# Gated decode attention: one ring for all loads, V as the stationary operand, and stages interleaved per 512 rows

## The chip, the cores and the metric

One core of a Trainium2 chip runs the kernel. A core has TensorE (PE: matmuls; its weight loads are listed as PEld), VectorE (DVE), ScalarE (ACT), GpSimd (POOL), SyncE (SP, which here issues the transfers) and 16 DMA engines. The metric is the device time of one execution in microseconds. No other core runs. The profile also gives TensorE's granted clock as a share of full speed. Ratios below are the record's ratios of fast runs with their 95% intervals, so they are not quite the ratio of the medians that are quoted.

## The reference, cut to what matters

```python
B, Sq, D = 2, 1, 448;  Hq, Hkv, Sk, Dh = 16, 8, 32768, 256;  F = 1792     # all bf16
q = (x @ wq) per head                                # one query row per batch entry
scores = einsum("bhqd,bhkd->bhqk", q, k) * Dh**-0.5  # two query heads share one K/V head
p = softmax(scores);  o = einsum("bhqk,bhkd->bhqd", p, v);  a = o @ wo
b = gelu(x @ w1 + b1) @ w2 + b2
g = sigmoid((x * gate_w).sum(-1));  out = g * a + (1 - g) * b
```

K and V are 268 MB each, and every byte is used once, for two query heads. So 537 MB must be moved, and TensorE must see all of it: K twice (a transpose, then the score product), V once. There are 16 groups (batch x K/V head) with 8 tiles of 4096 rows (2 MB) each of K and of V.

## The kernel before

A *step* takes one K tile through stages A and B, and one V tile, eleven steps behind, through stage C. Each stage runs over the whole tile before the next one begins.

```python
NBK = NBV = 4        # 4 buffers of 2 MB for K, 4 for V; wq, w1, w2 lie in V's at the start
NKT = 2; NPB = 3     # 2 buffers for a transposed K tile, 3 PSUM banks for transposes
...
def A(kt):                                   # 32 f32 transposes, two bf16 columns at a time
    wait_tile(E, ("K", kt))
    for bl in range(8):                      # 4 transposes to one bank, copied as 128x512
        E.wait(evac_eng(...), ("E", ...))    # the copy that empties this bank, ACT or DVE by turns
        for i in range(4): transpose(bank[:, i*P:(i+1)*P], KV[slot][:, r, :].bitcast(f32), ident_f)
def B(kt):                                   # 64 matmuls of 2 columns: KT is the weights
    for r in range(32):
        for j in range(2):
            matmul(pss[:, t*R + r, :], buf[:, j, r*P:(r+1)*P], qT_sb[:, kvh, j, :, b], ...)
def C(vt):                                   # 32 matmuls of 256 columns: P is the weights, V streams
    for r in range(32):
        matmul(ps_o[g % 2][0:2, 0:Dh], pt[:, t*R + r, :], KV[slot][:, r, :], ...)
...
for s in range(NSTEP + 1):
    A(s); B(s - 1); ...; C(s - DELTA)        # DELTA = 8 + 3
```

SyncE issues x (element by element), K tile 0, wq, K tile 1, the small weights and biases, then K and V tiles by turns, each when the last user of its buffer is done.

## Time and profile before

| | before |
|---|---|
| time, median of 4 | 1371.09 us (1369.15 to 1375.18); of the first 3, which the prediction knew, 1371.68; later medians of 7, 1369.57 to 1371.15 |
| profiled span | 1367.6 us |
| PE busy, granted clock | 93%, 0.980 |
| transfers | 549.8 MB, mean 402 GB/s |
| PE waiting for a transfer | 17 us, all before 50 us (14.5 for K, 1.7 for the gate weights, 1.0 for wq) |

These lines are from the profile's page of the kernel before. PE and PEld give busy time. The rows of 40 digits are equal slices of the span: the granted clock in tenths, the busy share of the DMA engines, and GB/s. Then follow the chain of waits by engine (it goes back from the last instruction, at each step to what released it), and the costliest groups of instructions with busy time, mean ns of one, and idle time ahead of them.

```profile
span 1367.6 us, 36510 instructions
...
PE 1269.7 (93%) x16778; PEld 1035.4 (76%) x16778; DVE 682.2 (50%) x1144; ACT 564.4 (41%) x1126; POOL 1.2 (0%) x9
...
PEclk7899999999999999999999999999999999999999
DMA  8989999999999999999999999999999999999876
GB/s 277 414 356 427 426 426 426 427 426 425 413 415 407 407 419 404 420 413 415 401 402 419 407 419 417 407 419 409 405 409 410 418 405 414 427 426 425 338 272 289
...
PE 73%; DVE 12%; ACT 10%; SPq 2%; issue 1%; DMA 1%; DVEq 0%
...
L414 PE MATMUL psT<-ident_f,KV 128*128 128x128 f32 x4096 | 565.3, 282 | 90.9 <-ACT KT L596 39.6
...
L477 PE MATMUL ps_o<-KV,PT 128*2 128x256 bf16 x4096 | 480.1, 277 | 0.0
...
L440 PE MATMUL ps_s<-qT_sb,KT 128*128 128x2 bf16 x8192 | 223.0, 163 | 0.0
```

All of DMA reads 9 tenths and so does PE, so neither row says which of them is the limit. The chain does: 73% PE, 22% copies, 1% DMA. The next lines are the chain in order of time for one step (start, duration, what):

```profile
212.34 0.60 PE psT L414 x4
...
212.96 1.08 ACT KT L596 x2
...
216.13 1.09 PE psT L414 x8
217.22 1.58 PE ps_s L440 x64
218.80 3.58 PE ps_o L477 x32
222.38 0.60 PE psT L414 x4
```

Transposes and the copies that they wait for take 4.9 us, scores 1.6, the value product 3.6; the step is 10.04 us. The windows of the same kernel (stretch, its length, busy time with count on PE, PEld, DVE, ACT and POOL, clock, DMA share, GB/s):

```profile
120.00:200.00 80.00, 75.35 (x1023) 61.82 (x1021) 42.48 (x71) 34.85 (x69) 0.00 (x0) 1.00 1.01 425
400.00:800.00 400.00, 377.31 (x5039) 307.95 (x5038) 207.09 (x347) 169.46 (x337) 0.00 (x0) 0.99 1.00 411
```

425 GB/s were moved from 120 to 200 us, and 411 later (413 from 800 to 1200 us).

### The profile page before, as it was taken

What the parts mean: (1) busy time and instruction counts of PE and PEld (TensorE: products, weight loads), DVE (VectorE), ACT (ScalarE), POOL (GpSimd) and SP (SyncE); (2) the same over time, 40 slices, a digit from 0 to 9 for tenths busy, and PEclk for the clock granted to TensorE, in tenths of its full rate; (3) what the DMA queues carried; (4) which work ended last, traced back from release to release, by engine and by line L of the source; (5) the groups of instructions that cost most, each with busy time, mean ns of one, the idle gap of its engine ahead of it and who ended that gap; (6) DMA issues with size and microseconds to landing.
All of it is one profiled execution on the core that took longest, in us unless ns stands there. A gap on an engine that the chain in (4) does not pass through costs nothing.

```text
span 1367.6 us, 36510 instructions
## 1 busy us (share of the span) xinstructions
PE 1269.7 (93%) x16778; PEld 1035.4 (76%) x16778; DVE 682.2 (50%) x1144; ACT 564.4 (41%) x1126; POOL 1.2 (0%) x9
## 2 busy tenths in 40 slices
PE   5898999999999999999999999999999999999998
PEld 5777777777777777777777777777777777777776
DVE  1575455455445545545545545455445545545520
ACT  2555344444434434444334434344344434444410
POOL 0000000000000000000000000000000000000000
PEclk7899999999999999999999999999999999999999
DMA  8989999999999999999999999999999999999876
GB/s 277 414 356 427 426 426 426 427 426 425 413 415 407 407 419 404 420 413 415 401 402 419 407 419 417 407 419 409 405 409 410 418 405 414 427 426 425 338 272 289
DMA packets 47664, 549.78 MB, mean 402 GB/s; under 512 B 7508, under 2 KB 13400, under 8 KB 14744
## 3 DMA queue, kind: packets, MB, share of 16 engines
q1 hardware_dynamic: 47512, 547.45, 97.1%
q8 instruction: 132, 2.16, 0.6%
q14 instruction: 20, 0.16, 0.0%
HBM read 547.43 MB, written 0.00 MB: 400 GB/s over the span
## 4 chain that ended last, share of the span: by engine, by line
PE 73%; DVE 12%; ACT 10%; SPq 2%; issue 1%; DMA 1%; DVEq 0%
PE ps_o L477 34%; PE psT L414 22%; PE ps_s L440 14%; DVE KT L666 12%; ACT KT L596 10%; DMA KV<-in_A_k_cache_dram 1%; SPq L270 1%; PE ps_m L492 1%; PE ps_s L504 0%; PE ps_m L451 0%; SPq L266 0%; PE ps_m L458 0%; PE ps_s L389 0%; ACT z_sb L577 0%; SPq L259 0%
## 5 line engine op out<-in xcount | busy, mean ns | idle before, releaser
L666 DVE COPY KT<-psT 128x512 bf16<-128x512 bf16 x1024 | 647.0, 685 | 546.1 <-PE psT L414 534.3
L596 ACT COPY KT<-psT 128x512 bf16<-128x512 bf16 x1024 | 537.9, 595 | 713.8 <-PE psT L414 713.6
L414 PE MATMUL psT<-ident_f,KV 128*128 128x128 f32 x4096 | 565.3, 282 | 90.9 <-ACT KT L596 39.6
L414 PEld LDWEIGHTS psT<-ident_f,KV 128*128 128x128 f32 x4096 | 443.1, 142 | 206.9 <-DVE KT L666 95.7
L477 PE MATMUL ps_o<-KV,PT 128*2 128x256 bf16 x4096 | 480.1, 277 | 0.0
L477 PEld LDWEIGHTS ps_o<-KV,PT 128*2 128x2 bf16 x4096 | 340.6, 85 | 108.0 <-DMA KV<-in_A_v_cache_dram 0.2
L440 PEld LDWEIGHTS ps_s<-qT_sb,KT 128*128 128x128 bf16 x8192 | 223.5, 96 | 1.7 <-issue 0.2
L440 PE MATMUL ps_s<-qT_sb,KT 128*128 128x2 bf16 x8192 | 223.0, 163 | 0.0
L687 DVE RECIPROCAL rl<-ps_m 2x1 f32<-2x1 f32 x16 | 2.5, 156 | 100.3 <-PE ps_m L486 100.3
L608 ACT ACTIVATE PT<-ps_s,negm 128x256 bf16<-128x256 f32 x32 | 16.4, 541 | 0.5
L603 ACT ACTIVATE negm<-ps_m 128x2 f32<-128x2 f32 x16 | 2.8, 172 | 32.6 <-PE ps_m L458 32.6
L672 DVE TENSOR_REDUCE mx<-ps_s 128x2 f32<-128x512 f32 x16 | 11.1, 692 | 9.9 <-PE ps_s L440 9.9
L492 PE MATMUL ps_m<-ident_f,o_sb 2*128 2x2 f32 x64 | 9.6, 251 | 1.7 <-DVE o_sb L689 1.7
L677 DVE TENSOR_REDUCE gmax<-ps_m 2x1 f32<-2x128 f32 x16 | 4.5, 279 | 12.4 <-PE ps_m L451 12.4
L361 PE MATMUL ps_s<-xTa,KV 128*128 128x2 bf16 (+1 forms) x128 | 9.1, 173 | 1.0 <-DMA KV<-in_A_wq_dram 1.0
L696 DVE CAST attnT<-ps_m 128x2 bf16<-128x2 f32 x32 | 3.7, 157 | 12.9 <-PE ps_m L492 12.9
L492 PEld LDWEIGHTS ps_m<-ident_f,o_sb 2*128 2x128 f32 x64 | 8.3, 185 | 2.2 <-DVE o_sb L689 1.9
L361 PEld LDWEIGHTS ps_s<-xTa,KV 128*128 128x128 bf16 (+1 forms) x128 | 8.1, 104 | 2.2 <-DMA KV<-in_A_wq_dram 1.1
L689 DVE TENSOR_SCALAR o_sb<-ps_o,rl 2x256 f32<-2x256 f32 x16 | 7.5, 471 | 0.6
L504 PE MATMUL ps_s<-wo_sb,attnT 128*2 128x448 bf16 x32 | 6.4, 352 | 0.3 <-DVE attnT L696 0.3
L451 PE MATMUL ps_m<-ident_f,mx 128*2 128x128 f32 x32 | 6.3, 281 | 0.0
L458 PE MATMUL ps_m<-diag,ones_f 2*128 2x2 f32 x32 | 6.1, 256 | 0.0
(39 smaller groups left out, 47.2 us busy)
## 6 DMA issues: line engine op xcount, KB each, us to landing
KV<-in_A_k_cache_dram SPq DMA_DIRECT2D x128, 2048.0 KB, 10.7
KV<-in_A_v_cache_dram SPq DMA_DIRECT2D x128, 2048.0 KB, 10.4
wo_sb<-in_A_wo_dram SPq DMA_DIRECT2D x1, 3584.0 KB, 19.7
KV<-in_A_wq_dram SPq DMA_DIRECT2D x2, 1536.0 KB, 14.4
KV<-in_B_w_dram SPq DMA_DIRECT2D x1, 1568.0 KB, 11.0
KV<-in_B_w_dram SPq DMA_DIRECT2D x1, 1344.0 KB, 8.1
KV<-in_A_wq_dram SPq DMA_DIRECT2D x2, 256.0 KB, 15.4
KV<-in_B_w_dram SPq DMA_DIRECT2D x1, 224.0 KB, 7.6
```

The source lines that it names most:

```text
L270: dma(lambda e, b=b: e.dma_start(b2_bf[b:b + 1, :], B_b2.rearrange("(o k) -> o k", o=1)), "d_b", ("b2", b))
L361: E.ins(lambda e, cbase=cbase, half=half, kc=kc, kn=kn, kvh=kvh, sub=sub, hh=hh: e.matmul(ps_qT[:, kvh, sub, hh, :], wq_h[half][0:kn, kc, ...
L414: E.ins(lambda e, bank=bank, i=i, slot=slot, r=r: e.transpose(bank[:, i * P:(i + 1) * P], KV[slot][:, r, :].bitcast(dt.float32), ident_f[: ...
L440: E.ins(lambda e, pss=pss, t=t, r=r, j=j, buf=buf, kvh=kvh, b=b: e.matmul(pss[:, t * R + r, :], buf[:, j, r * P:(r + 1) * P], qT_sb[:, kvh ...
L477: E.ins(lambda e, pso=pso, slot=slot, r=r, pt=pt, t=t, first=first, last_grp=last_grp: e.matmul(pso, pt[:, t * R + r, :], KV[slot][:, r, : ...
L492: E.ins(lambda e, j=j: e.matmul(ps_m[:, C_OT[g % 2] + 2 * j:C_OT[g % 2] + 2 * j + 2], o_sb[g % 2][0:2, j * P:(j + 1) * P], ident_f[0:2, 0: ...
L504: E.ins(lambda e, c=c, kvh=kvh, hh=hh, j=j: e.matmul(ps_a, attnT[:, kvh, hh, j, :], wo_sb[:, c, :], start=(c == 0), stop=(c == NCH - 1)), ...
L596: E.ins(lambda e, sub=sub: e.copy(buf[:, sub, r0 * P:(r0 + 4) * P], bankv[:, sub, :]), key=(("E", kt, bl) if sub == 1 else None))
L608: E.ins(lambda e, hh=hh: e.activation(pt[:, :, hh], pss[:, :, hh], ACTF.Exp, bias=negm[g % 2][:, hh:hh + 1], scale=SCALE, accum_out=lsum[g ...
L666: E.ins(lambda e, sub=sub: e.tensor_copy(buf[:, sub, r0 * P:(r0 + 4) * P], bankv[:, sub, :]), key=(("E", kt, bl) if sub == 1 else None))
L672: E.ins(lambda e: e.tensor_reduce(mx[g % 2][:, :], pss[:, :, :].rearrange("p n h -> p h n"), AX.X, ALU.max), key=("MX", g))
L689: E.ins(lambda e: e.tensor_scalar(o_sb[g % 2][:, :], ps_o[g % 2][0:2, 0:Dh], rl2[g % 2][:, 0:1], None, op0=ALU.mult), key=("OS", g))
```

## The change

The intent: take TensorE off the critical path, so that only the transfers limit. V becomes the weights of the value product (64 matmuls of 2 columns instead of 32 of 256, and the output needs no transposing); the stages are cut into *units* of 512 rows and interleaved, so that nobody waits for a PSUM copy; one ring of 11 slots serves K, V and all weights; weights and biases are loaded in contiguous pieces. The diff, cut to its core:

```diff
-    NBK = 4;  NBV = 4;  NKT = 2;  LAG = 3;  DELTA = NT + LAG
+    BR = 4;  UNITS = NTILES * NBL
+    NB = 11;  LB = 2;  NKT = 5;  DELTA = NT + 2;  NPIECE = 4
...
-        KV = [sb(f"KV{i}", [P, R, Dh], dt.bfloat16) for i in range(NB)]
+        ring = sb("ring", [P, NB * SLOT], dt.bfloat16)
+        seq = [("WQ", 0)]            # then K(0), K(1), W1, W2, K(2) ... V(s-10), K(s+1) ...; WO near the end
...
-            dma(... A_wq[0:KCF * P, h * HDH:(h + 1) * HDH].rearrange("(kc p) n -> p kc n", p=P) ...)
+            o, src = view(d)[0:KP, :], A_wq.rearrange("(p k) n -> p (k n)", p=KP)      # KP = 112
...
-                for r in range(R):
-                    E.ins(lambda e, ...: e.matmul(
-                        pso, pt[:, t * R + r, :], KV[slot][:, r, :],
-                        start=first, stop=last_grp), ...)
+                for i in range(BR):
+                    for j in range(2):
+                        E.ins(lambda e, ...: e.matmul(
+                            ps_o[g % 2][:, 2 * j:2 * j + 2], kv[:, r, j * P:(j + 1) * P], pt[:, n, :],
+                            start=(n == 0 and j == 0), stop=(n == NT * R - 1), skip_group_check=True), ...)
...
-            for s in range(NSTEP + 1):
-                    A(s)
-                    B(s - 1)
-                    C(v)
+            do_QT()
+            for U in range(NSTEPU):
+                s, bl = divmod(U, NBL)
+                if U < UNITS:
+                    T(U)                       # 4 transposes
+                if 0 <= U - LB < UNITS:
+                    B(U - LB)                  # 8 score matmuls
+                ...
+                if 0 <= s - DELTA < NTILES:
+                    C(s - DELTA, bl)           # 8 value matmuls
```

## The prediction

> **What bounds the kernel now.** TensorE's own program, not the transfers, although both look full. The chain of waits gives PE 73%, DVE 12%, ACT 10%, DMA 1%; in the list of waits PE waits for K three times (18 us, all before 50 us) and practically never for V. One step (a 2 MB K tile and a 2 MB V tile) in the chain by time, from 212.3 us: transposes and the PSUM copies that they wait for 4.9 us, scores 1.6, value product 3.6, together 10.05 us; with the per-group work 10.2 us on average. 4.19 MB / 10.2 us = 411 GB/s, as the windows show from 400 to 1200 us. From 100 to 350 us, where the buffers were still filling, they show 426 to 428: the transfer limit is close behind, 4.9 us per tile, 9.83 per step. [...]this trace tops out at 429.
>
> **What the change does.**
> - Value product: 32 matmuls of 256 moving columns (3.6 us) become 64 of 2 columns with V as weights. The score stage has that form: 64 in 1.6 to 1.74 us, 27 ns each[...]. Saves 1.9 us per step.
> - Interleaving hides the 2.4 us of copies on the chain. VectorE needs 4 x 1.29 = 5.2 us per step, ACT 4.3: both fit.
> - TensorE's step becomes 3.7 to 4.1 + 1.7 + 1.7 = 7.3 us, with switching and waits an estimated 8.5 at most. That is under 9.83: DMA-bound.
> - One ring of 11 instead of 4+4: K-only and V-only phases may use all slots, so transfers need not stop at either end. Now the last 100 us run at 337, 271 and 287 GB/s and the third slice at 356.
> - Start: the first large load is issued at 3.0 us, behind four transposed x loads; after, at 0.7. The element-wise bias loads (13.9 us of issue) go. Query weights come before K, so the first transpose starts near 20 us instead of 11, and the first ten steps are TensorE-bound (6 us per K tile against 4.9), but eleven slots absorb that lag.
> - Tail after the last landing: 0.9 us of products, multiplies, four matmuls 0.9, mix 0.7, output 1.5.
>
> **Sum.** 549.8 MB plus 0.3 MB of instructions at 426.5 GB/s = 1290 us; first bytes near 2.5; tail 5: span about 1298. The timed median lies 4.1 us over the profiled span: **1302 us**, 5.1% less. TensorE's chain loses about 128 x 2.6 = 330 us, but only 70 can be had, because the transfers take over.
>
> Range (8 in 10) 1294 to 1328. Chances: faster by over 2% 0.94, within 2% 0.05, slower 0.01.
>
> **What would show it.** Right: 425 to 428 GB/s in nearly every slice, PE 75 to 85% busy and waiting for DMA every step, copies gone from the chain, products at 27 ns spacing. Wrong: a step still near 10 us with PE not waiting for DMA (switching between f32 transposes and bf16 products, or slower weight loads from V); about 410 GB/s with PE waiting (426 not sustainable); queue gaps in the first 100 or last 60 us.
>
> **What would make it wrong.** TensorE pauses every step once it waits for DMA; the granted clock, which dips to 0.91 in some 20 us windows, could fall further, though a slow TensorE stops pausing. Loads into 112 partitions may run below full rate (a few us).

1290 for the transfers, 2.5 and 5 make a span of about 1298, and 4.1 more make 1302 us. The 8.5 us per step at most is an estimate with no trace behind its 1.2 us for switching and waits. Two of its readings need care. The 18 us of waits for K count one wait of 3.4 us twice, for PE and for its weight loads; PE itself waited 14.5 us, in two waits. And 429 GB/s is the highest of the windows of 20 us; shorter ones go higher, to 446 in one of 5 us.

## The result, and the profile after

The kernel became slower: 1434.14 us median (1430.83 to 1437.27, 4 runs), ratio 1.0454 (95% interval 1.0428 to 1.0480). The page of the kernel after, the same parts as above:

```profile
span 1433.8 us, 45406 instructions
...
PE 1400.0 (98%) x20810; PEld 1319.8 (92%) x20810; DVE 683.5 (48%) x1136; ACT 570.2 (40%) x1109; POOL 1.2 (0%) x9
...
PEclk9796555555555555555555555555555555555555
DMA  9999999999999999999999999999999999999986
GB/s 294 426 426 425 424 426 427 424 426 400 388 386 384 391 370 378 395 371 387 362 390 388 374 381 371 389 392 364 389 371 390 378 375 389 376 385 368 386 318 268
...
PE 96%; DMA 3%; DVE 1%; issue 0%; ACT 0%; SPq 0%; ACTq 0%
...
L351 PE MATMUL psT<-ident_f,ring 128*128 128x128 f32 x4096 | 1080.3, 417 | 10.5 <-DMA ring<-in_A_k_cache_dram 9.8
...
L370 PE MATMUL ps_s<-qT_sb,KT 128*128 128x2 bf16 x8192 | 403.5, 171 | 1.7 <-DVE KT L468 1.1
L412 PE MATMUL ps_o<-PT,ring 128*128 128x2 bf16 x8192 | 350.6, 165 | 0.6 <-issue 0.6
```

The line to see is PEclk. TensorE runs at half clock from the fifth slice to the end (mean 0.538) while it is 98% busy, and its weight loads are 92% busy against 76% before. The chain is 96% PE: the copies are gone from it, as predicted, but a transpose now counts 417 ns instead of 282. The windows of the kernel after: a stretch before the clock fell, one after it, and a long one.

```profile
103.30:113.80 10.50, 10.50 (x243) 10.32 (x241) 7.73 (x12) 6.43 (x13) 0.00 (x0) 1.00 1.00 424
123.00:133.90 10.90, 10.90 (x168) 10.40 (x165) 5.15 (x8) 4.29 (x8) 0.00 (x0) 0.50 1.00 425
400.00:800.00 400.00, 400.00 (x5802) 379.74 (x5799) 191.55 (x317) 160.38 (x313) 0.00 (x0) 0.50 0.96 382
```

In the first line 243 matmuls are recorded in 10.5 us, in the second 168 in 10.9 us, with PE busy to 100% in both. A unit took 0.875 us at full clock (a step 7.0 us; the prediction said 7.3) and takes 1.36 us at half clock (a step 10.9 us, longer than the 10.04 of before). The moment of the fall, in the timeline of PE (start, duration, instructions; in brackets the idle time before, and what ended it):

```profile
118.07 0.44 PE L351 MATMUL psT<-ident_f,ring 128*128 128x128 f32 x2 [0.74 <-issue]
...
119.62 0.67 PE L351 MATMUL psT<-ident_f,ring 128*128 128x128 f32 x4
...
120.56 1.09 PE L351 MATMUL psT<-ident_f,ring 128*128 128x128 f32 x4
```

One pause of 0.74 us, for which the profile shows no cause ("issue"), at 117.3 us; at 120.1 us the clock record goes to 0.50. PE has no pause from then to 1400 us, and the clock stays at 0.50 for 1293.7 us, until the matmuls of 448 columns of the output product at 1409 us bring it back for 6.8 us (1413.7 to 1420.6). In the traces of before and after the clock record shows 0.50 and 1.00 alone; the dips to 0.91 over 20 us in before are single pieces of 3.4 us at 0.50 (eight of them from 340.5 us on). TensorE had not begun to wait for transfers each step; the prediction's DMA-bound state was never reached.

### The profile page after: what moved, and what is told of

It reads as the page before. It is cut to its first block, busy times and chain, and to the rows that moved or that the text cites. A ratio compares the mean times of both kernels' runs of the same rounds, so it can differ in the third digit from the quotient of the medians.

```text
span 1433.8 us, 45406 instructions
## 1 busy us (share of the span) xinstructions
PE 1400.0 (98%) x20810; PEld 1319.8 (92%) x20810; DVE 683.5 (48%) x1136; ACT 570.2 (40%) x1109; POOL 1.2 (0%) x9
## 4 chain that ended last, share of the span: by engine, by line
PE 96%; DMA 3%; DVE 1%; issue 0%; ACT 0%; SPq 0%; ACTq 0%
PE psT L351 64%; PE ps_o L412 15%; PE ps_s L370 13%; DMA ring<-in_A_k_cache_dram 3%; PE psT L421 1%; PE ps_m L379 1%; PE ps_m L384 1%; PE ps_m L389 0%; DVE KT L468 0%; PE ps_o L327 0%; PE ps_o L336 0%; SPq L296 0%; ACT PT L497 0%; DVE mx L555 0%; ACT KT L466 0%
## 5 line engine op out<-in xcount | busy, mean ns | idle before, releaser
L351 PE MATMUL psT<-ident_f,ring 128*128 128x128 f32 x4096 | 1080.3, 417 | 10.5 <-DMA ring<-in_A_k_cache_dram 9.8
L468 DVE COPY KT<-psT 128x512 bf16<-128x512 bf16 x1024 | 659.2, 685 | 697.5 <-PE psT L351 696.6
L466 ACT COPY KT<-psT 128x512 bf16<-128x512 bf16 x1024 | 549.8, 589 | 810.4 <-PE psT L351 810.4
L351 PEld LDWEIGHTS psT<-ident_f,ring 128*128 128x128 f32 x4096 | 708.2, 210 | 11.6 <-DMA ring<-in_A_k_cache_dram 10.0
L370 PEld LDWEIGHTS ps_s<-qT_sb,KT 128*128 128x128 bf16 x8192 | 459.1, 114 | 65.8 <-DVE KT L468 5.4
L370 PE MATMUL ps_s<-qT_sb,KT 128*128 128x2 bf16 x8192 | 403.5, 171 | 1.7 <-DVE KT L468 1.1
L412 PE MATMUL ps_o<-PT,ring 128*128 128x2 bf16 x8192 | 350.6, 165 | 0.6 <-issue 0.6
L412 PEld LDWEIGHTS ps_o<-PT,ring 128*128 128x128 bf16 x8192 | 294.2, 104 | 7.8 <-issue 7.5
L497 ACT ACTIVATE PT<-ps_s,negm 128x256 bf16<-128x256 f32 x32 | 16.6, 545 | 0.5
L555 DVE TENSOR_REDUCE mx<-ps_s 128x2 f32<-128x512 f32 x16 | 10.9, 680 | 0.5 <-PE ps_s L370 0.5
L421 PE MATMUL psT<-ring,attnT 128*2 128x448 bf16 x32 | 9.3, 464 | 0.3 <-DVE attnT L575 0.3
L389 PE MATMUL ps_m<-lsum,ones_f 128*128 128x2 f32 x32 | 8.9, 348 | 0.4 <-ACT PT L497 0.4
```

What stands on the lines that cost most here:

```text
L351: E.ins(lambda e, bank=bank, i=i, kv=kv, r=r: e.transpose(bank[:, i * P:(i + 1) * P], kv[:, r, :].bitcast(dt.float32), ident_f[:, :]), key ...
L370: E.ins(lambda e, pss=pss, n=n, i=i, j=j, buf=buf, kvh=kvh, b=b: e.matmul(pss[:, n, :], buf[:, j, i * P:(i + 1) * P], qT_sb[:, kvh, j, :, ...
L389: E.ins(lambda e: e.matmul(ps_m[:, C_L:C_L + 2], ones_f[:, :], lsum[g % 2][:, :], start=True, stop=True), key=("L", g))
L412: E.ins(lambda e, g=g, kv=kv, r=r, n=n, j=j, pt=pt: e.matmul(ps_o[g % 2][:, 2 * j:2 * j + 2], kv[:, r, j * P:(j + 1) * P], pt[:, n, :], st ...
L421: E.ins(lambda e, c=c, kvh=kvh, hh=hh, j=j: e.matmul(ps_a, attnT[:, kvh, j, hh, :], wo_v[:, c, :], start=(c == 0), stop=(c == NCH - 1)), k ...
L466: f = lambda e, j=j: e.copy(buf[:, j, :], bankv[:, j, :])
```

## The experiments

The theories at the outset:

- **A**: the clock grant follows how much of TensorE's time is *wide streaming*. Matmuls of 2 columns keep PE busy in the profile but do not count. The old value product (256 columns, 3.6 of every 10 us) had been paying for the clock.
- **B**: cutting the work into short pieces drops the clock, whatever the pieces are.
- **C**: a wait for a transfer drops it, whatever the work.
- **D**: the array or its weight loads do too much, and that holds the clock down.

| run | what differs | us, median | ratio to before (95%) | clock |
|---|---|---|---|---|
| after | | 1434.14 | 1.0454 (1.0428 to 1.0480) | 0.538 |
| e1_wide_v | after, V streams again | 1387.69 | 1.0140 (1.0119 to 1.0160) | 0.994 |
| e2_narrow_v_alone | before, V as weights | 1336.78 | 0.9765 (0.9744 to 0.9786) | 0.741 |
| e3_dose4 | after + 4 useless wide matmuls per unit | 1334.86 | 0.9749 (0.9732 to 0.9767) | 0.953 |
| e3_dose2 | after + 2 of them | 1332.83, one run | none | 0.849 |
| e4_one_burst | after + one burst | 1416.19 | 1.0335 (1.0308 to 1.0363) | 0.560 |
| e5_narrow_dose | after + 8 useless narrow ones per unit | 1673.05, one run | none | 0.532 |
| e6_coarse | after, whole-tile stages | 1331.21 | 0.9722 (0.9696 to 0.9748) | 0.755 |
| e7_dose2_wo_contig | e3_dose2, other load of wo | 1331.27 | 0.9718 (0.9703 to 0.9733) | 0.850 |
| e8_dose2_chunked | e3_dose2, other loads of wq, w1 | 1332.80 | 0.9720 (0.9701 to 0.9739) | 0.843 |
| e9_light_c | after, a quarter of the value product | 1323.98 | 0.9648 (0.9627 to 0.9669) | 0.692 |
| e10_coarse_chunked | e6_coarse, loads of e8 | 1329.88 | 0.9695 (0.9674 to 0.9716) | 0.757 |

All gave the correct result except e7 and e9, which are wrong.

### e1: undo the form of V alone

```diff
-  for j in range(2): matmul(ps_o[g%2][:, 2*j:2*j+2], kv[:, r, j*P:(j+1)*P], pt[:, n, :])
+  matmul(ps_o[g%2][0:2, 0:Dh], pt[:, n, :], kv[:, r, :])
```

> The kernel after with one part undone: the value product is again 32 matmuls of 256 moving columns per tile (P as weights), everything else (ring, interleaving, loads) stays. Theory A (the clock grant follows how much of the array's time is wide streaming, and 2-column products do not count): the granted clock stays at 0.95 or more, PE's step is 3.7 + 1.7 + 3.6 = 9.0 us, under the transfer's 9.83, so 420 to 427 GB/s and about 1302 us. Theory B (cutting the stages into pieces of 4 transposes with short products between them drops the clock, whatever the form of V): the clock stays near 0.54 and the time is 1430 us or more. Theory C (the first wait for a transfer drops the clock, whatever the work): near 0.54 too.

The clock is 0.994: from 55.7 us to the end it never falls. Theory B is out: the pieces are as short as in the kernel after. Theory C is not tested here, since PE waits for a transfer only near the start:

```profile
PE psT L353 <- DMA ring<-in_A_k_cache_dram: 9.8, 2, 8.7
```

C is out by the kernel after itself, whose clock fell at 120.1 us with no wait for a transfer since 45 us. This run leaves a rival: from 56 to 1381 us PE has no pause over 0.35 us, so the clock may have held because nothing paused and not because V streams. Two other traces speak against that. The kernel before paused for 2.15 us at 110.4 us, between long blocks of transposes and 5 us before its first product of V, and kept the full clock until 340.5 us: that pause alone did not drop it; and after the fall, with no pause at all, the kernel after did not get it back.

The time is 1387.69 us, not 1302: 1.4% over before, clear of noise. PE's timeline of one unit:

```profile
701.26 0.66 PE L353 MATMUL psT<-ident_f,ring 128*128 128x128 f32 x4
701.76 0.34 PE L372 MATMUL ps_s<-qT_sb,KT 128*128 128x2 bf16 x8
702.03 0.60 PE L421 MATMUL ps_o<-ring,PT 128*2 128x256 bf16 x4
702.56 0.66 PE L353 MATMUL psT<-ident_f,ring 128*128 128x128 f32 x4
```

The unit is 1.30 us at full clock (701.26 to 702.56 for the next transposes), some 10.3 us per step. I had expected 9.0 from adding the stages' own times. From start to start, the four transposes take 0.50 us, the eight scores 0.27 us, and the four wide products 0.53 us; inside the long blocks of before, eight scores take 0.20 us (64 in 1.58) and four wide products 0.45 (32 in 3.58). So in this run the short stages of different kinds did not keep the pace of the long blocks, and interleaving with a wide V hid the copies, and gave that back at the seams.

### e2: the form of V alone, in the kernel before

```diff
-  matmul(pso, pt[:, t*R + r, :], KV[slot][:, r, :])
+  for j in range(2): matmul(ps_o[g%2][:, 2*j:2*j+2], KV[slot][:, r, j*P:(j+1)*P], pt[:, t*R + r, :])
```

> The kernel before with one part of the change alone: V as stationary operand (64 matmuls of 2 columns per tile), stages still one whole tile long, old buffers and loads. Theory A: clock well under the 0.98 of before (0.5 to 0.8; the transposes come as one block of about 5 us, so it may come back for a part of each step), and a time of 1370 to 1480 us in spite of 1.9 us less TensorE work per step. Theory B: clock stays at 0.97 or more, step 8.2 us, DMA-bound, 1300 to 1320 us. Theory C: the clock falls at the first wait and stays down.

Theory A had the clock right (0.741) and the time wrong: 1336.78 us, 2.3% *faster* than before. PE's timeline:

```profile
706.00 6.35 PE L414 MATMUL psT<-ident_f,KV 128*128 128x128 f32 x32 [0.19 <-DMA KV<-in_A_k_cache_dram]
712.19 1.74 PE L440 MATMUL ps_s<-qT_sb,KT 128*128 128x2 bf16 x64
713.79 1.80 PE L478 MATMUL ps_o<-PT,KV 128*128 128x2 bf16 x64
715.89 6.38 PE L414 MATMUL psT<-ident_f,KV 128*128 128x128 f32 x32 [0.30 <-DMA KV<-in_A_k_cache_dram]
```

The block of transposes begins at half clock each step (32 of them take 6.35 us where before took about 4.9), gets the clock back within the block, and the scores and products then run at full speed. A step is 9.9 us and PE ends it with a wait for K (0.19 and 0.30 us in these lines), so the transfers are the limit. One part of the change alone is a gain. PE waits for transfers here (50 times), and the clock comes back in nearly every step (100 times from 150 to 1200 us); theory C had it fall at the first wait and stay down.

### e3: add useless wide work to the kernel after

```diff
+  for _ in range(4):                       # 2 in the second version
+      matmul(bank[:, 0:128], ident_b, ident_b)    # overwritten by the transposes below
   for i in range(BR): transpose(bank[:, i*P:(i+1)*P], ...)
```

> The kernel after with work added: four useless bf16 matmuls of 128 moving columns ahead of the four transposes of each unit of 512 rows (into the bank that the transposes then overwrite), 4096 in all, 0.22 us per unit at full clock. Theory A: the clock comes back (0.9 or more) and the kernel gets faster by adding work: unit 0.88 + 0.22 = 1.10 us, step 8.8 us, DMA-bound, about 1302 us. Theory D (the clock is held down because the array or its weight loads do too much[...]): the clock stays at 0.5 or lower and the time rises by 1024 x 0.43 = 440 us at half clock.

> As the run with four, with two useless matmuls per unit, to find how much is enough. Theory A: between the two: either the clock comes back (about 1302 us) or it stays near 0.5 and the step is 10.9 + 8 x 0.21 = 12.6 us, about 1640 us. Theory D: 1434 + 220 us.

With four, 4096 matmuls whose result is thrown away make the kernel 7% faster than the kernel after: 1334.86 us at clock 0.953. Two per unit are enough (1332.83 us, a single run, clock 0.849; e8, which has the same two, was timed four times at 1332.80). D is out: with more work in the array the clock is higher (0.849 and 0.953 against 0.538). Lines of the page with four (the clock by slices, and the chain by engine):

```profile
PEclk9799999999999998998999998999999799999865
...
DMA 59%; PE 38%; issue 1%; SPq 1%; DVE 0%; ACT 0%; ACTq 0%
```

And its largest wait of PE, which was nowhere in the kernel after (us in total, times, longest):

```profile
PE ps_o L414 <- DMA ring<-in_A_v_cache_dram: 105.0, 78, 9.2
```

This is the state that the prediction described, TensorE waiting for V and transfers in the lead, but at 1333 us and not at 1302.

### e5: the control for e3

```diff
+  for _ in range(8): matmul(bank[:, 0:2], ident_b, ident_b[:, 0:2])
```

> Control for the runs with useless work: eight useless matmuls of 2 moving columns per unit in the same place (about 0.21 us per unit, as much TensorE time as four of 128 columns at full clock). Theory A (only wide streaming earns the clock): clock stays near 0.54, the unit is 1.36 + 0.21 us, about 1434 + 1024 x 0.21 = 1650 us. Rival (any extra TensorE work, or the later start of the transposes, brings the clock back): 0.85 or more and about 1335 us.

One of its windows, far into the run:

```profile
300.00:400.00 100.00, 100.00 (x1761) 95.60 (x1760) 41.37 (x69) 34.55 (x68) 0.00 (x0) 0.50 0.84 328
```

Eight narrow useless matmuls cost time and earn nothing: 0.50 from 101.1 us on, but for 6.8 us near the end, and 1673.05 us (one run). The start of the run says the same: there, with no product of V yet, the kernel after earned the full clock at 55.2 us with transposes and scores alone; with the eight narrow ones in each unit it kept the pace of half clock (four transposes in 1.09 us, against 0.64 later) until the 14 matmuls of 448 columns of w2 (71.4 to 75.3 us) brought it, at 73.8 us. So it is neither extra TensorE work nor the shifted start of the transposes that brings the clock back in e3, but the wide columns.

### e4: one burst

```diff
+  for _ in range(64 if U == 560 else 0): matmul(bank[:, 0:128], ident_b, ident_b)
```

> The kernel after with one single burst of 64 useless matmuls of 128 moving columns at unit 560 (near 780 us; 6.8 us at half clock), nothing else. Theory A1 (narrow work can hold the full clock once it is granted, as it did from 56 to 118 us; a pause of TensorE in a wait for a transfer drops it, and at half clock this work never earns it back): the clock is 0.50 before the burst, 1.00 for about 100 us after it (the ring is about 4 steps ahead; a step takes 7.1 us against 9.83 us of transfers, so it is empty after 14 steps), then TensorE waits for a transfer, and the clock is 0.50 to the end. Time: 14 x (10.9 - 7.1) = 53 us gained, 7 lost, about 1388 us. Theory A2 (narrow work cannot hold the clock at all): back to 0.50 within 20 us, 1430 to 1440 us.

Windows before and within the full-clock stretch:

```profile
700.00:750.00 50.00, 50.00 (x726) 47.83 (x725) 23.34 (x38) 18.78 (x36) 0.00 (x0) 0.50 0.97 380
750.70:788.20 37.50, 35.90 (x782) 34.76 (x780) 24.25 (x42) 20.72 (x42) 0.00 (x0) 1.00 0.97 400
```

The burst brings the full clock back at 750.7 us, and the narrow work, with nothing added, holds it for 37.5 us (782 matmuls recorded, where the same 37.5 us have some 545 at the pace of the line before); then it is gone for 604 us. That speaks in outline for the form of theory A (A1) in which the same work can hold the clock and cannot earn it (forecast 1388 us, measured 1416.19). Two details of the expectation failed. The stretch was 37.5 us and not 100, and a wait for a transfer did not end it. PE's timeline has these pauses in the stretch, and a third of 0.25 us between them:

```profile
767.38 0.33 PE L353 MATMUL psT<-ident_f,ring 128*128 128x128 f32 x1 [0.40 <-issue]
...
786.25 0.19 PE L414 MATMUL ps_o<-PT,ring 128*128 128x2 bf16 x2 [0.90 <-issue]
```

The clock fell at 788.2 us, after the last of them. All the falls into a lasting half clock that I looked up come within 3 us of such a pause: 0.74 us before 120.1 us in the kernel after, 0.71 before 143.1 and 0.90 before 788.2 in e4, 0.98 before 101.1 in e5. Pauses of 0.25 to 0.42 us in the same stretches were survived, and, among long blocks of transposes, the 2.15 us of before. That is an observation in a few places, not an experiment; what causes the pauses is open.

### e6: undo the interleaving alone

```diff
-    NB = 11;  LB = 2;  NKT = 5;  DELTA = NT + 2
+    NB = 10;  LB = 8;  NKT = 16; DELTA = NT + 4
-    per unit: T(U); B(U - LB); C(s - DELTA, bl)
+    per step: T of all 8 units; B of all 8; C of all 8
```

> The kernel after with the interleaving undone and nothing useless added: per step all 8 units of transposes in one block, then 64 score matmuls, then 64 value matmuls (this takes 16 KT buffers, so the ring has 10 slots, and the value product runs 12 tiles behind instead of 10). Theory A with windows ([...]one block of 5 us of transposes per step earns the clock back, and the same work cut into pieces of 0.4 us does not): clock 0.7 to 0.8 as in the run with narrow V alone, DMA-bound, 1320 to 1345 us. If the order of the work does not matter, only its sum: clock near 0.54 and 1430 us.

1331.21 us at clock 0.755, as the first theory of the expectation forecast, and 7% under the kernel after, with the very same matmuls in another order. Three successive windows of a step, 3.4 us each:

```profile
700.00:703.40 3.40, 3.09 (x58) 2.63 (x57) 3.30 (x6) 2.57 (x5) 0.00 (x0) 1.00 0.97 414
703.40:706.80 3.40, 2.84 (x97) 2.75 (x94) 1.16 (x2) 0.00 (x0) 0.00 (x0) 0.98 1.04 443
706.80:710.20 3.40, 3.40 (x19) 3.33 (x18) 1.81 (x3) 2.15 (x4) 0.00 (x0) 0.52 0.99 414
```

The window from 706.8 us is almost all transposes at half clock (19 matmuls recorded, PE busy throughout); the next one is granted full speed. The same transposes cut into pieces of four, with scores and products of V between, did not earn it from 120 to 1409 us in the kernel after; with the scores alone between they did, at 55.2 us. So the cause is a *pair*: narrow V takes the wide work away, and the transposes that are left were not granted the clock in pieces of four per 1.36 us (0.50), while in blocks of 32 they were (e2 0.741, e6 0.755). Either half alone leaves enough of the clock here: e1 keeps 0.99 (with no pause to test it, and a time 1.4% over before), e2 and e6 recover in nearly every step. The page of this run (clock by slices; chain by engine):

```profile
PEclk9799777777776777876677776776678866787755
...
DMA 52%; PE 41%; issue 3%; DVE 2%; SPq 1%; ACT 1%; ACTq 0%
```

### The other 31 us: what the transfers can sustain

The prediction took 426.5 GB/s as the sustained rate. In e3_dose2, 33 slices do show 424 to 427 GB/s, but the last three 309 to 355:

```profile
GB/s 291 418 425 425 424 424 426 424 425 426 425 424 426 425 425 424 427 425 424 425 426 424 426 426 424 425 425 425 424 425 425 425 424 426 426 422 414 355 311 309
```

I first blamed the load of wo, which comes just there in 4096 pieces of 896 bytes.

```diff
-    o, src = wo_v, A_wo.rearrange("(c p) n -> p c n", p=P)
+    o, src = view(d), A_wo.rearrange("(p c) n -> p (c n)", p=P)
```

> The kernel with two useless wide matmuls per unit (1333 us, DMA-bound) with the load of wo made contiguous per partition (128 pieces of 28 KB instead of 4096 of 896 B); the result is wrong on purpose. If the 896-byte load is what holds the transfers at half their engines (share 0.5, about 210 GB/s) for 20 us near the end, that stretch goes and the time falls by 9 to 13 us to about 1321 us. If the stretch comes from slots or from a slow TensorE in the tail, nothing changes (1333 us).

It was a miss: 1331.27 us, what the expectation gave for a lack of slots or a slow TensorE in the tail. The low stretch did not go; it moved to the very end:

```profile
GB/s 288 416 425 426 423 426 425 425 424 427 423 425 426 425 426 424 427 424 426 425 424 426 424 426 425 425 425 425 425 425 424 425 426 425 425 423 418 404 414 166
```

So the time went to another place and was not saved. The trace has the landing of each transfer as 16 separate increments of its semaphore. Worked out from them, in us (mean time between successive tiles from 120 to 1000 us, for the last and for the first of the 16 increments, and the distance of the last from the first near three times):

```
                 per tile, last   per tile, first   spread at 300 / 600 / 1000
before           5.073            5.073             5.3 /  1.8 /  2.6
after            5.363            5.381             7.5 /  1.2 /  2.5
e2_narrow_v_alone 5.016           4.890             6.4 / 14.2 / 24.0
e3_dose2         5.024            4.889             8.7 / 16.5 / 27.5
e6_coarse        5.015            4.890             8.7 / 16.4 / 25.7
e9_light_c       4.980            4.892             9.7 / 14.2 / 22.0
```

In the four runs of the table that wait for transfers, these drift apart: the spread is 22 to 27.5 us at 1000 us. The fastest part of a tile lands every 4.89 us, the slowest every 5.02 (4.98 in e9). My reading, which fits the 424 to 427 GB/s of the slices and the 309 to 355 of the last three: while the fast ones may still run ahead through the ring, the bytes moved per us look like 426 GB/s; but a tile can be used only when its last part is there, and at the end the fast ones have nothing left. For 256 tiles, 5.024 instead of the 4.916 that 426.5 GB/s stands for is 28 us. In the kernels that TensorE limits the spread is 1.2 to 2.6 us at 600 and 1000 us; that the fast ones are held back there is again my reading. And the 425 GB/s of before from 120 to 200 us did not show the pace of whole tiles either (spread 5.3 us near 300): complete tiles came every 4.99 us in that window, not every 4.92.

```diff
-  for i in range(BR):                      # value product of a unit
+  for i in (BR - 1,):
```

> The kernel after with only one of four row blocks in the value product (wrong result on purpose, 12,288 TensorE instructions fewer, fewer instruction packets: some 115 instead of 163), so that TensorE is under the transfers' pace at either clock. What is disputed is the floor of the transfers. In the DMA-bound runs the 16 engines drift apart by about 1.5 us every 50 us, to 30 us and more at the end, so that a tile is complete every 5.045 us and not every 4.92. Theory E (16 engines of unequal pace set the floor, whatever TensorE does): 1325 to 1333 us, the landings of one tile spread over about 30 us at the end. Theory F (the drift comes from instruction packets that some engines carry): spread about 21 us and 1320 to 1327 us. If instead TensorE's own half-clock stretches held the other runs, the floor is lower: 1300 to 1310 us.

The expectation calls engines what the trace shows as 16 increments, and its 5.045 us per tile and 1.5 us of drift per 50 us are 5.015 to 5.024 and 1.2 to 1.3 in the table above (e2, e3_dose2, e6, the drift from 300 to 1000 us). Measured: 1323.98 us, a spread of 22 us near 1000 and 25 near 1170, and 4.980 us per tile: the time is in theory F's range and 1 us under theory E's, the spread a little over F's 21. The instruction packets (the page counts them beside those of the loads, as packets of the kind "instruction") fell from 163 in the kernel after to 115. The slowest pace minus the fastest is nearly proportional to these packets in all DMA-bound runs, 0.75 to 0.79 ns per tile and packet. It is 0.088 us with 115 packets (e9), 0.125 with 163 (e6), 0.126 with 164 (e2), 0.135 with 179 (e3_dose2) and 0.154 with 195 (e3_dose4). So e9 keeps 71% of the packets of e6 and 70% of its drift. That favours F for the whole drift, but it is a correlation: no run changes the packets alone, and e9 also asks less of TensorE. TensorE's half-clock stretches are not what sets the floor: with TensorE this light and the clock at 0.69, the time is still far over 1310. How the packets would slow some parts and not others is open: near 1000 us in e3_dose2, eight of the 16 increments come 25 to 28 us after the first and six within 1.5 us.

```diff
-    A_wq.rearrange("(p k) n -> p (k n)", p=KP)
+    A_wq.rearrange("(k p) n -> p k n", p=KP)          # w1 likewise; x transposed to match
```

> The kernel with two useless wide matmuls per unit (1333 us, DMA-bound), with the loads of the query weights and w1 cut into pieces of one row (8 KB and 3.5 KB) instead of one contiguous piece of 32 KB and 14 KB per partition. In the trace of after the 32 KB packets took 1980 ns (16.5 GB/s per engine) and the 14 KB ones 920 ns (15.6), while the 4 KB rows of the same weights in before took 159 ns (25.8) and the 16 KB ones of K 611 ns (26.8). If the long pieces are what is slow, the query weights land near 12 us instead of 17.7 and the run ends 5 to 8 us earlier, 1325 to 1328 us. If it is the 112 partitions or the cold start, nothing changes.

> The coarse version (stages of one tile, nothing useless, 1331 us) with the same row-wise loads: the best version that I know. 5 to 8 us under the coarse run if long pieces are slow: 1323 to 1327 us; otherwise 1331.

Both missed. The query weights landed at 18.1 us (17.7 with long pieces) and e8 took 1332.80 us. The 8 KB pieces of wq moved at about the same 16 GB/s per engine as the 32 KB ones (in the first 17 us, 229 GB/s at a DMA share of 0.92 in e8 and 240 at 0.91 in the kernel after: 15.6 and 16.5). So the length of the pieces is not what makes the first 17 us run at 230 to 240 GB/s. A cold start does not show: in before, the first 128 packets of K (16 KB, from 4.2 us) took 611 ns as later ones did, and in the kernel after the 14 KB packets of w1 were slow still at 26 to 34 us (920 ns, 15.6 GB/s). wq and w1 cover 112 partitions; w2, which covers 128, moved its 12.25 KB packets at 26.0 GB/s (482 ns, 32 to 39 us). That the 112 partitions are the cause is a candidate that no run tests. e10 is the fastest correct version, 3.0% under before, but its interval overlaps that of e6: the loads gained nothing that can be told from noise.

## Why the prediction was wrong, point by point

- *"What bounds the kernel now. TensorE's own program"*: right for the clock of 0.98, by the chain. But the margin was smaller than I thought: the transfers' pace for whole tiles is 5.02 us, and the kernel before took 5.07.
- *"64 in 1.6 to 1.74 us, 27 ns each"* and *"7.3 us"* per step: right at full clock. The kernel after ran a step in 7.0 us from 103 to 113 us.
- *"Interleaving hides the 2.4 us of copies on the chain"*: right; the copies are at 0 to 1% of the chain after, and at 0% in e3_dose4 with the clock at 0.953.
- *"a slow TensorE stops pausing"*: **this is the step that failed.** I had seen the clock dip to 0.91 (340 to 380 us in before) and argued that a slow TensorE gets busy, and a busy TensorE gets its clock back; the second half was my assumption, which no trace showed. On it rested the step cost, *"7.3 us, with switching and waits an estimated 8.5 at most. That is under 9.83: DMA-bound"*, which is a cost at full clock. At half clock the step took 10.9 us, over the 9.83 of the transfers, and PE was busy without a pause from 120 to 1400 us and did not get its clock back. Being busy was not enough: adding wide work cured it (e3, 0.953), adding the same time of narrow work did not (e5, 0.532), and undoing either the narrow V or the fine interleaving cured it (e1 0.994, e6 0.755). It cost 101 us: 1434 against 1333 with the same kernel and two useless matmuls per unit.
- *"549.8 MB plus 0.3 MB of instructions at 426.5 GB/s = 1290 us"*: a term of the sum that was mis-sized, though hidden by the first failure. The rate of bytes moved was not the rate at which tiles become complete: 5.02 us per tile instead of 4.92, 28 us in 256 tiles. So the runs here that wait for transfers end at 1324 to 1337 us.
- *"first bytes near 2.5"* with query weights at full rate: the first 17 us ran at 240 GB/s, and the query weights landed at 17.7 us; at 426.5 GB/s 3.67 MB would have taken 8.6 us and landed near 11. About 6 us of the sum.
- *"Loads into 112 partitions may run below full rate"*: these two did (15.6 and 16.6 GB/s per packet in the kernel after, against 26.0 and 26.7 for w2 and K over 128 partitions); the cause is not shown.
- *"eleven slots absorb that lag"*: right; the rate was 424 to 427 GB/s in slices 2 to 9.
- Queue gaps at the end, named as a sign of being wrong: they appeared in the DMA-bound runs. The drift accounts for the pace before them (5.02 us per tile); but in e3_dose2 SyncE also waits 37.3 us for a free slot there, and no run has more slots, so what these gaps cost is open.

## What to carry to other kernels

Before narrowing a matmul to save TensorE time, ask which instructions stream many columns, and how close together those that remain will come. Here a TensorE that was 98 to 100% busy, with 2-column matmuls between short transposes, sat at half clock for 1294 us. Busy time does not tell the two clocks apart, for weight loads no more than for matmuls: they were 98% busy from 103.3 to 113.8 us at full clock, and 95% from 123.0 to 133.9 at half. If the clock is lost, try the cheap cures and measure: longer stages (a whole tile instead of 512 rows: clock 0.755, 1331 us), or a few useless wide matmuls (two of 128 columns per unit: 0.849, 1333 us). And take a transfer limit from the time between *complete* tiles over the whole run (5.02 us here), not from GB/s in a stretch where the faster transfers may be running ahead (4.92 us at 426.5 GB/s).
